# A recurrent attention and rational MLP kernel: first ScalarE activation made a reciprocal root, and a new order table

## The chip, the cores and the metric

The program runs on one core of one Trainium2 chip. The metric is device microseconds of one execution, the median of several. Every engine of the core (TensorE, VectorE, ScalarE, GpSimd, SyncE; in the rows PE, DVE, ACT, POOL, SP) works through its own list of instructions in order and waits on semaphores for the others.

## The reference

A gated linear recurrence over 768 steps for 4 batches of 8 heads of 48, and then an MLP with a rational function on its 3072 rows of 384:

```python
for t in range(S):
    state = alpha[:, :, t, :, None] * state + np.einsum('bhd,bhe->bhde', k[:, :, t], v[:, :, t])
    y[:, :, t] = np.einsum('bhd,bhde->bhe', q[:, :, t], state)
...
h = x @ w_in
h2 = h * h
h3 = h2 * h
P = a[0] + a[1] * h + a[2] * h2 + a[3] * h3
Q = 1.0 + np.abs(b[0]) * np.abs(h) + np.abs(b[1]) * h2
g = P / (Q + 1e-06)
return (g @ w_out).astype(np.float32)
```

The weights arrive as 64-bit floats and are turned into 32-bit ones on the chip.

## The kernel before

The 3072 tokens are cut into 24 blocks g of 128 for the recurrence and into 6 groups of 512 for the MLP, which does 96 jobs u: 10 small early ones on 256 tokens ("plain") and 86 wide ones, each of one slice of 128 of the 2048 hidden columns.

All work is split into 2672 steps. Each is recorded with an engine and with the steps that it must follow; the table ORDER then gives one sequence for all engines, and a bit in each entry moves a step to its other engine where it has one. No engine reorders its list, so a step that waits holds up all that stand behind it on that engine.

The steps that the prediction speaks of, by the names in the code:

- Loads on SP: `nat` (the first four blocks of alpha, k, q, 384 KB each for a pair of blocks), `w` (one of 16 tiles of weights, 768 KB), `ld` (from block 4 on: alpha, k or q of one block in four quarters, each two transfers of 48 KB into one buffer for alpha, `raw_a`, and one for k and q, `raw_qk`), `v`. The built program gives the transfers eight semaphores in turn, so a transfer is issued only when the one eight places ahead of it has landed. The notes of the change call this the ring.
- Weights: `low` and `join` on DVE, `abs` and `sign` on ACT (or POOL, DVE) turn a tile's 64-bit words into 32-bit floats.
- Recurrence of block g: `tn` (PE turns the loaded data) and `cp` (ACT copies it to SBUF) for the first four blocks; `ta` (alpha) and `tqk` (k and q), transposes on DVE, for the others; they free the one buffer for the next block's `ld`. Then `suf`, `inv`, `pre` (scans on DVE), `k` and `q` (products on POOL or DVE), `s` (scores, PE), `se` (ACT), `sm` (POOL), `kt` (PE), `ke` (ACT), `am` (PE), `kv` (DVE), `xh` and `xl`.
- MLP job u: `in` (PE, two halves 0 and 1), `ah`, `t1`, `q1` (ACT; `q1` also POOL), `qm` (POOL), `t2`, `t3` (DVE), `ars` (ACT, the reciprocal root, L755), `sq` (ACT), `p`, `t`, `g` (DVE, the last is L771), `gh` (ACT), `gl` (POOL or DVE), then `oh` and `ol` (PE). `in` of job u writes the PSUM bank that job u-3 used, so it must follow `g` of job u-3.
- `prime` (ACT) is an activation on one column whose result nobody uses. `one_eps`, its input, is a column that POOL sets at the start.

Of the kernel before, what the change touches and what calls it, by code (L numbers as in the profile page):

```python
# [24 lines left out]
class Plan:  # L25
# [52 lines left out]
    '^&j=3^D2}IP&mz_sW^#>tGnv8ilB*9LPgRvY^HLllIpUW96X<@si`!I+Nl}XM@^yOw15J1O-;v{IGU!>7+OSM)hw)`N~',
    'ytWA<f3=)I$AGH3QYvSbD4q(hQn|x7Ay<gr2EFG?QAY#k7`|(mOSa7U4bhLKUWQw2ao#OZ7^<SAA7;^<CXjv+09cP90P',
    '$wTEh{74%%Kr;WjLaRYT!n`sk0RiD*L+DlJVdo>T|(0trN-_%^%M<diKIuJZWEx<QwHT6?NRk+$p3$d&Er%uyi?4&-aG',  # L80
    'qi@b(SF)a{nZzBhz`;YI!sIOw;HC3&|kHa&Jx2%g>Zz<(NX%Pg4HehPwgTFw`qWi3g?55QBk@;$EmaG5{L#P)kPYp?$8',
    'R{O(#eI;E#Gqmq<fOhz{M=aCMI^Qy_4K3`BvG^os7%Ra%NY)K9exAJ8=lQm5!XC4g?~HC?BN^oV}Y4f61Ye$rza6nIO^',
    'k)WpvQK=wOg{mj?o*blsl~{~=sdsdf62VjYMTymKiUBd<8GWFSlo(>cCwfkCA&DwZ7LvecN(*sdl=?%x14$tTMBx{dG!',
    'T`)&?<}vUnwk*jHB^C`bMcCIxCLFF*rH@rPT<G92;Wt8q5aqA+;(DvAG~51mcXqycXkd0a%A|IXQf%^(dTzQ*sVY2Jv_',
    'Urs2#=b9}a3f^tAkPRj{673YKqRgw&+QMn)?=jL4OxD<O%&G|STXMn7b4)Q~3PRzL>J!jx;n1mB?+CU!8$YnVn<mZi8h',
    'BI*%m6tbRAxO$uRUIzJ1$YZ?#tK{pMysuunG14VF3;PsB9Bp7xDw}9S-B8rfy|JN3v*>IMTJ!nF3Jr!J6GYVkO@jtRo;',
    'PJxjr}Kv4LV-oQtT&oF2MyHEzQ7xExgH65NQJau3c9&A2=?=kDBs|KsXV0ZKv*E*fabCAk#z=E^EB4CmHRlY4S49?v5<',
    'z{Q~kjO1S2hg)$TsLdhVnuEA6PvAD(kK1xJs0jTznD^mC9>67_imC~dxEM_4fm{@(@J=iO?RX(i<tnfXL%Ab&=G{1r_h',
    '1;8hDE#=^Qb{Qox{03ci|aaHLxECa|AbnNS?`~cnOz<A-tG3^H9zkXbZD=>B!l<g_m<1IDm7w3=QL>yp>1u3T~{LKvUS',
    'pwP7bO<72pz>%kaq1#@{7kL7WEj92q^Zlc!k4z2|Aco)}&`Fw(#!2&+crPW$4OU>aVU+2?&hAYE5KE(}SH}ByMTt>BrI',  # L90
    '&cv8@_IhY`*<VY;D&IH_j5Za8>j`FxM|=Jp63JH18(t4zQ7l`KHTKHe4Fp^5q!l*@g85|gCk#aW4O<U_zgec+UhsI=ZA',
    'cl2f-u$!-w%LAK^OcI9}!t{FpoNKkfoo809ZVmv>w@@R5~}T;=ZYiJ$NZ1o_M{WGIxQFZ`8RM4oai=>^wVOK&hT5Uiw>',
# [1079 lines left out]
```

## Time and profile before

| | us |
|---|---|
| median of 3 runs | 535.96 |
| lowest and highest | 534.93 to 538.28 |
| the profiled execution, device time | 537.53 |
| its span, first to last instruction | 535.8 |

The rows further down come from the profiled execution, and their times count from the start of its span. Its device time is 1.7 us longer than its span, and 1.57 us over the median. TensorE's granted clock was 0.997 of full speed over the span.

### The profile page before, as it was taken

How to read it: one execution, taken by the hardware profiler on the slowest of the kernel's cores; microseconds unless marked ns; L12 is line 12 of the kernel's file. 1: busy time of each engine (PE TensorE's matmuls, PEld its weight loads, DVE VectorE, ACT ScalarE, POOL GpSimd, SP SyncE). 2: the span in 40 equal slices, each digit the busy share in tenths (PEclk: the TensorE clock that was granted, in tenths of full speed). 3: DMA queues.
4: the chain of work that ended last, by engine and by line, in shares of the span. 5: the costliest groups of instructions: out<-in, count | busy, mean ns of one | idle time of the engine just before them, and what ended most of it. 6: DMA issues, size and time to landing. Idle time of an engine off the chain costs nothing.

```text
span 535.8 us, 11861 instructions
## 1 busy us (share of the span) xinstructions
PE 517.1 (97%) x4342; PEld 428.1 (80%) x4342; DVE 480.7 (90%) x716; ACT 430.2 (80%) x730; POOL 392.4 (73%) x387
## 2 busy tenths in 40 slices
...
GB/s 246 260 249 219 214 229 116 116 140 113 128 140 117 92 127 71 104 96 109 92 68 87 112 73 94 97 87 59 128 95 55 88 83 18 1 40 1 59 1 62
DMA packets 146174, 57.46 MB, mean 107 GB/s; under 512 B 133056, under 2 KB 138688, under 8 KB 146112
## 3 DMA queue, kind: packets, MB, share of 16 engines
...
## 4 chain that ended last, share of the span: by engine, by line
PE 70%; SPq 7%; DMA 7%; DVE 6%; POOL 4%; ACT 3%; issue 2%; DVEq 0%; POOLq 0%; ACTq 0%
PE ps L670 29%; PE ps L689 23%; PE ps L683 6%; PE ps L547 5%; SPq L402 4%; PE ps L505 3%; DMA wo_words<-in_moe_w_out_dram 2%; DMA raw_a<-in_alpha_dram 2%; PE ps L656 1%; SPq L409 1%; DMA tv<-in_v_dram 1%; POOL gh_gl L778 1%; PE ps L523 1%; PE ps L566 1%; DVE t L748 1%
## 5 line engine op out<-in xcount | busy, mean ns | idle before, releaser
L670 PE MATMUL ps<-x,wi 128*128 128x512 f32 x774 | 209.1, 396 | 3.7 <-DVE t L771 3.7
L689 PE MATMUL ps<-gh_gl,wo 128*128 128x512 f32 x630 | 176.5, 400 | 0.1
L670 PEld LDWEIGHTS ps<-x,wi 128*128 128x128 f32 x774 | 143.8, 188 | 36.1 <-ACT ah L725 3.0
L737 POOL TENSOR_TENSOR qm<-qm,ah 128x512 f32<-128x512 f32 x96 | 124.2, 1295 | 24.7 <-ACT qm L734 14.7
L689 PEld LDWEIGHTS ps<-gh_gl,wo 128*128 128x128 f32 x630 | 115.5, 188 | 27.6 <-DVE parts L704 0.5
L778 POOL TENSOR_TENSOR gh_gl<-t,gh_gl 128x512 fp32r<-128x512 f32 x74 | 96.2, 1301 | 16.4 <-ACT gh_gl L774 6.3
L728 ACT ACTIVATE t<-ps,coef 128x512 f32<-128x512 f32 x96 | 74.5, 776 | 21.2 <-PE ps L670 12.8
L755 ACT ACTIVATE ps<-qm,one_eps 128x512 f32<-128x512 f32 x96 | 66.3, 691 | 20.5 <-POOL qm L737 11.9
L732 POOL TENSOR_SCALAR qm<-ah,bab 128x512 f32<-128x512 f32 x62 | 47.8, 771 | 47.4 <-ACT ah L725 22.5
L762 DVE SCALAR_TENSOR_TENSOR t<-t,coef,ps 128x512 f32<-128x512 f32 x96 | 71.0, 739 | 12.6 <-ACT ps L758 11.7
L748 DVE TENSOR_TENSOR t<-t,ps 128x512 f32<-128x512 f32 x96 | 65.1, 678 | 11.3 <-ACT t L728 5.6
L752 DVE SCALAR_TENSOR_TENSOR t<-t,coef,ps 128x512 f32<-128x512 f32 x96 | 71.3, 744 | 2.5 <-ACT ah L725 0.7
L725 ACT ACTIVATE ah<-ps 128x512 f32<-128x512 f32 x96 | 57.0, 593 | 17.7 <-PE ps L670 12.0
L771 DVE SCALAR_TENSOR_TENSOR t<-ps,t 128x512 f32<-128x512 f32 x96 | 66.1, 688 | 1.9
L765 DVE SCALAR_TENSOR_TENSOR ps<-qm,ps 128x512 f32<-128x512 f32 x96 | 66.0, 688 | 0.0
L774 ACT ACTIVATE gh_gl<-t 128x512 fp32r<-128x512 f32 x86 | 53.7, 628 | 9.2 <-DVE t L771 7.3
L758 ACT ACTIVATE ps<-ps 128x512 f32<-128x512 f32 x96 | 56.1, 585 | 2.0
L488 POOL TENSOR_TENSOR tqk<-tqk,tg 128x512 f32<-128x512 f32 x21 | 27.2, 1294 | 13.4 <-DVE tg L461 7.7
L491 POOL TENSOR_TENSOR tqk<-tqk,fp 128x512 f32<-128x512 f32 x21 | 27.2, 1295 | 12.6 <-DVE wo_words L274 5.0
L516 POOL TENSOR_SCALAR_AFFINE_SELECT sc<-sc 128x1024 f32<-128x1024 f32 x24 | 26.2, 1092 | 13.2 <-ACT sc L512 4.0
L461 DVE TENSOR_TENSOR_SCAN tg<-ta,ps 128x528 f32<-128x528 f32 x24 | 29.8, 1244 | 6.5 <-ACT ta L445 6.5
L683 PE MATMUL ps<-wo,gh_gl 128*128 128x384 f32 x180 | 35.5, 337 | 0.0
...
## 6 DMA issues: line engine op xcount, KB each, us to landing
...
wi_words<-in_moe_w_in_dram SPq DMA_DIRECT2D x8, 768.0 KB, 6.9
wo_words<-in_moe_w_out_dram SPq DMA_DIRECT2D x8, 768.0 KB, 7.0
...
```

Of the source, the lines that this page charges most:

```text
L670: nc.tensor.matmul(h_of(u), w(key)[:, kt * FU + f % FU, :], x[:, kt, xp, :], start=(n == 0), stop=(n == len(todo) - 1),)
L683: nc.tensor.matmul(bank(T_BANKS[tt], DM), g[:, tt * P : (tt + 1) * P], w(("o", f // FU))[:, f % FU, :], start=(f == 0 and first_w), stop=( ...
L689: nc.tensor.matmul(bank(O_BANKS[dt]), w(("o", f // FU))[:, f % FU, dt * P : (dt + 1) * P], g, start=(f == 0 and first_w), stop=(f == NF - ...
L728: nc.scalar.activation(buf(s, "t1", u), h_of(u), AF.Identity, bias=a2, scale=a3)
L737: nc.gpsimd.tensor_tensor(buf(s, "qm", u), buf(s, "qm", u), buf(s, "ah", u), op=ALU.mult)
L748: nc.vector.tensor_tensor(t, t, h_of(u), op=ALU.mult)
L752: nc.vector.scalar_tensor_tensor(t, t, a1, h_of(u), op0=ALU.add, op1=ALU.mult)
L755: nc.scalar.activation(h_of(u), buf(s, "qm", u), AF.Abs_reciprocal_sqrt, bias=one_eps)
L762: nc.vector.scalar_tensor_tensor(t, t, a0, h_of(u), op0=ALU.add, op1=ALU.mult)
L765: nc.vector.scalar_tensor_tensor(h_of(u), buf(s, "qm", u), 1.0 + 1e-6, h_of(u), op0=ALU.add, op1=ALU.mult)
L771: nc.vector.scalar_tensor_tensor(t, h_of(u), 2.0, t, op0=ALU.subtract, op1=ALU.mult, reverse0=True)
L778: eng.tensor_tensor(buf(s, "gl", u).rearrange("p a b -> p (a b)"), buf(s, "t1", u), gh, op=ALU.subtract)
```

## The change

`prime` becomes the function that `ars` uses, in place of a copy, and the four kinds of ACT steps that can come early (`bab`, `abs`, `sign` and `cp`) are now recorded as following it. The table is new: every engine's list is in another order, and 90 steps are on another engine than before.

```diff
 ORDER = [
-    'c-jTQ17ICU6ac_|TGh5~+qP}n_VqVuSlhO3+qP}n?aho+O2t*N)f6>RMOCPrnxI5QQC^K#anw{5T`f?H)k-y8O;eN9WH',
...
+    'c-jrs1Cu7a5<uZ}r#tCnZQHhO+qP|g`_9ac*0yciwr$%s?)?j=o~omiQ&AMFaVoBgtx!!-(bWWHlvh#Jc(p*qP!rWO6-UK',
...
-    add("bab", "ACT", 0.2, abs_coef, (), ["coef"])
+    add("bab", "ACT", 0.2, abs_coef, (), ["coef", "prime"])
...
-    add("prime", "ACT", 1.5, nc.scalar.activation, (first_act, one_eps, AF.Copy), ["one_eps"])
+    add("prime", "ACT", 1.5, nc.scalar.activation, (first_act, one_eps, AF.Abs_reciprocal_sqrt), ["one_eps"])
...
-        add(("abs", key), "ACT", 0.94, join_scale, (key, n), [("w", key)] + [("join" if kept(x) else "lo", x) for i, x in enumerate(keys[:n]) if wr_slot(i) == wr_slot(n)][-1:], alt=("POOL", 2.22, False))
+        add(("abs", key), "ACT", 0.94, join_scale, (key, n), [("w", key), "prime"] + [("join" if kept(x) else "lo", x) for i, x in enumerate(keys[:n]) if wr_slot(i) == wr_slot(n)][-1:], alt=("POOL", 2.22, False))
...
-        add(("sign", key), "ACT", 1.95, join_sign, (key,), [("low", key)], alt=("DVE", 1.04, True))
+        add(("sign", key), "ACT", 1.95, join_sign, (key,), [("low", key), "prime"], alt=("DVE", 1.04, True))
...
-                        [("tn", m, nm, x) for x in range(2) if par in (None, x)] + into[nm])
+                        [("tn", m, nm, x) for x in range(2) if par in (None, x)] + into[nm] + ["prime"])
```

The lines of the changed file are one lower than those of the file before (L770 there is L771 here).

**ScalarE at the start.** Before, the list begins with the load of a function table and the copies of what PE has turned. A second table load stands before the first `ars`.

```order
L445 ACT_TABLE_LOAD
L445 ACTIVATE ta0_82<-ps_69 128x4x128
L445 ACTIVATE ta1_83<-ps_69 128x4x128
L445 ACTIVATE tqk0_88<-ps_69 128x512 x2
L445 ACTIVATE tqk1_89<-ps_69 128x512
```

Now `prime` (L62) is first, and the list has this one table load and no other:

```order
L62 ACT_TABLE_LOAD
L62 ACTIVATE first_act_75<-one_eps_73 128x1
L444 ACTIVATE ta0_82<-ps_69 128x4x128
L444 ACTIVATE ta1_83<-ps_69 128x4x128
L444 ACTIVATE tqk0_88<-ps_69 128x512
L444 ACTIVATE tqk1_89<-ps_69 128x512
```

The table load stood behind a wait for PE's first turned data, and now stands ahead of all of it.

**VectorE around `ta` of block 7.** Before, from `pre` of block 6 on (`ta1` is the tile of block 7, `tqk0` that of block 6, `t11` and `t12` the working tiles of jobs 7 and 8; L453 is `ta`, L458 `tqk`, L771 `g`):

```order
L473 SCALAR_TENSOR_TENSOR fp0_84<-ta0_82,ps_69 128x528
L762 SCALAR_TENSOR_TENSOR t11_106<-t11_106,coef_71,ps_69 128x512
L748 TENSOR_TENSOR t12_107<-t12_107,ps_69 128x512
L765 SCALAR_TENSOR_TENSOR ps_69<-qm1_109,ps_69 128x512
L453 STREAM_TRANSPOSE ta1_83<-raw_a0_80 128x4x2x2x32
L771 SCALAR_TENSOR_TENSOR t11_106<-ps_69,t11_106 128x512
L752 SCALAR_TENSOR_TENSOR t12_107<-t12_107,coef_71,ps_69 128x512
L458 STREAM_TRANSPOSE tqk0_88<-raw_qk0_81 128x16x2x32
```

Now, from `g` of job 7 on (L770 is `g`, L457 `tqk`, L452 `ta`):

```order
L770 SCALAR_TENSOR_TENSOR t11_106<-ps_69,t11_106 128x512
L751 SCALAR_TENSOR_TENSOR t12_107<-t12_107,coef_71,ps_69 128x512
L457 STREAM_TRANSPOSE tqk0_88<-raw_qk0_81 128x16x2x32
L273 TENSOR_SCALAR wo7_words_983<-wo7_words_983 128x768
L293 SCALAR_TENSOR_TENSOR parts_76<-parts_76,wi7_words_828 128x768
L293 SCALAR_TENSOR_TENSOR parts_76<-parts_76,wo5_words_904 128x768
L761 SCALAR_TENSOR_TENSOR t12_107<-t12_107,coef_71,ps_69 128x512
L747 TENSOR_TENSOR t10_105<-t10_105,ps_69 128x512
L764 SCALAR_TENSOR_TENSOR ps_69<-qm0_108,ps_69 128x512
L751 SCALAR_TENSOR_TENSOR t10_105<-t10_105,coef_71,ps_69 128x512
L770 SCALAR_TENSOR_TENSOR t12_107<-ps_69,t12_107 128x512
L452 STREAM_TRANSPOSE ta1_83<-raw_a0_80 128x4x2x2x32
```

`ta` of block 7 stood ahead of `g` of job 7 and now follows `g` of job 8, eleven steps later.

**SyncE between two weight tiles.** Before, from `w` o1 to `w` o2:

```order
L257 DMA wo_words<-in_moe_w_out_dram 128x2x768
L402 DMA raw_qk_81<-in_k_dram 32x4x96 x2
L402 DMA raw_a_80<-in_alpha_dram 32x4x96 x6
L402 DMA raw_qk_81<-in_k_dram 32x4x96 x2
L257 DMA wo_words<-in_moe_w_out_dram 128x2x768
```

Now, from `w` o1 on:

```order
L256 DMA wo_words<-in_moe_w_out_dram 128x2x768
L448 DMA tv_93<-in_v_dram 128x8x48
L253 DMA wi_words<-in_moe_w_in_dram 128x3x512
L401 DMA raw_a_80<-in_alpha_dram 32x4x96 x2
L401 DMA raw_qk_81<-in_k_dram 32x4x96 x2
L401 DMA raw_qk_81<-in_q_dram 32x4x96 x2
L256 DMA wo_words<-in_moe_w_out_dram 128x2x768
```

Ten small transfers stood between these two weight tiles; now, from `w` o1 to `w` i7, no more than six stand between two. Further on, `w` o7 and o5 stood between the loads of block 5 and those of block 6's k and q; now o5 stands ahead of the first of block 6's k and q and o7 behind the first two quarters, and block 6's set is complete before any quarter but one of block 7's alpha. At the very start `w` i0 is the fourth transfer, ahead of `nat` of the second pair's alpha, where it was the fifth.

## Rows read from the trace of the kernel before

**Rows 1.** Page, busy time of each engine, its share and its instructions.

```profile
PE 517.1 (97%) x4342; PEld 428.1 (80%) x4342; DVE 480.7 (90%) x716; ACT 430.2 (80%) x730; POOL 392.4 (73%) x387
```

**Rows 2.** Busy time by stage; the first number after the stretch is its length.

```profile
9.10:43.00 33.90, 27.20 (x434) 25.21 (x432) 31.00 (x44) 27.66 (x44) 13.42 (x19) 0.95 0.94 255
43.00:107.00 64.00, 59.59 (x516) 49.19 (x517) 58.74 (x88) 57.61 (x78) 42.21 (x38) 1.00 0.67 177
107.00:164.00 57.00, 57.00 (x501) 46.11 (x501) 55.27 (x83) 53.34 (x89) 53.53 (x46) 1.00 0.52 126
164.00:245.00 81.00, 80.54 (x659) 64.56 (x658) 76.97 (x114) 66.31 (x118) 70.05 (x65) 1.00 0.44 103
245.00:529.00 284.00, 282.50 (x2167) 233.23 (x2166) 256.27 (x385) 222.38 (x401) 210.54 (x194) 1.00 0.31 67
```

**Rows 3.** PE, waits up to 107 us: total, times, longest.

```profile
PE ps L670 <- DVE t L771: 2.7, 1, 2.7
PE ps L547 <- ACT kt L526: 2.6, 1, 2.6
```

**Rows 4.** DVE, waits from 9.2 to 107 us.

```profile
DVE ta L453 <- DMA raw_a<-in_alpha_dram: 2.6, 1, 2.6
DVE tqk L458 <- DMA raw_a<-in_alpha_dram: 2.2, 1, 2.2
DVE st_s L576 <- PE ps L566: 1.4, 1, 1.4
DVE wi_words L294 <- ACT wr L266: 1.1, 1, 1.1
```

**Rows 5.** Timeline of ACT and DVE at the start: start, length.

```profile
7.14 1.28 ACT L445 ACT_TABLE_LOAD   x1 [7.14 <-PE ps L426]
8.43 1.09 ACT L445 ACTIVATE ta<-ps 128x512 f32<-128x512 f32 x2
9.12 2.40 DVE L461 TENSOR_TENSOR_SCAN tg<-ta,ps 128x528 f32<-128x528 f32 x2 [6.49 <-ACT ta L445]
```

**Rows 6.** Timeline of ACT at the first `ars`.

```profile
34.11 0.80 ACT L728 ACTIVATE t<-ps,coef 128x512 f32<-128x512 f32 x1
34.93 1.28 ACT L755 ACT_TABLE_LOAD   x1
36.22 0.69 ACT L755 ACTIVATE ps<-qm,one_eps 128x512 f32<-128x512 f32 x1
```

**Rows 7.** Timelines of DVE and PE around `ta` 7, `g` 7, `g` 9.

```profile
92.55 0.71 DVE L453 STREAM_TRANSPOSE ta<-raw_a 128x512 f32<-128x512 f32 x1 [2.62 <-DMA raw_a<-in_alpha_dram]
...
105.60 0.69 DVE L771 SCALAR_TENSOR_TENSOR t<-ps,t 128x512 f32<-128x512 f32 x1
...
93.99 1.41 PE L670 MATMUL ps<-x,wi 128*128 128x512 f32 x5 [2.65 <-DVE t L771]
...
106.49 0.73 PE L670 MATMUL ps<-x,wi 128*128 128x512 f32 x2
```

**Rows 8.** Groups by line: `gl`, `sign`, `q`, `k` on DVE, `q1` on ACT.

```profile
L734 ACT ACTIVATE qm<-ah,bab 128x512 f32<-128x512 f32 x34 | 27.6, 811 | 0.3
...
L778 DVE TENSOR_TENSOR gh_gl<-t,gh_gl 128x512 fp32r<-128x512 f32 x12 | 8.2, 684 | 1.0 <-issue 0.7 <-POOL sc L516 0.2
...
L280 DVE TENSOR_SCALAR wi_words<-wi_words 128x768 uint16<-128x768 uint16 x4 | 4.8, 1204 | 0.0
...
L491 DVE TENSOR_TENSOR tqk<-tqk,fp 128x512 f32<-128x512 f32 x3 | 3.2, 1053 | 0.0
...
L488 DVE TENSOR_TENSOR tqk<-tqk,tg 128x512 f32<-128x512 f32 x3 | 2.1, 690 | 0.1
```

**Rows 9.** The queue of SP: what its issues waited for, whole span.

```profile
SPq L402 <- DMA wo_words<-in_moe_w_out_dram: 8.9, 6, 3.5
```

**Rows 10.** Issues of 0 to 8 us: KB, us to landing.

```profile
wi_words<-in_moe_w_in_dram SPq DMA_DIRECT2D x1, 768.0 KB, 6.8
...
raw_second<-in_alpha_dram SPq DMA_DIRECT2D x1, 384.0 KB, 5.3
```

More of the change, by code (lines that the diff above doesn't have):

```diff
@@ L78 @@
[L78 to L92, printed above, removed]
@@ new lines @@
+    '6m$8q6X<oDn#c{1N1~Zt{SKjI;ZNUtEuj~e&DQ{jN$r%8mu3whN_1iq9b%MHC|7_o;shdp{}bdD!-nfd+E@SMk-7X)#ua=',
+    'Ra0eG!}LYfM-|YQRiyq;-&D8M2{lh2Q@PY6T|!O8`MQ}Jsf(-OdKOO9({KisQ~`Zojnbp_Oq{C6=*c0|ahkrSs;epbfhwh',
+    '@>vn2}?x$L)nR<a<6fzs1s#&_A9;?^t*Q$^nrx)ray05yeI;dBwy;`bg>vg)LTCC^bOI1sCQiIhp{Z_5l8$*`s@9Ld;q8_',
+    'U~dX6rv_v*WWJ8FdvQk(R9wNl?x&(vJKL4QzlvANo;SLv4Oo9e8dtD&k(U=hAh{nZw|PjA)p@Q3=UPU~&@K*$+AA4P?zR_',
+    'dVstoG~GdVpGhZ`2|EQEk_2^bXxs4N(j6upXv%>a!YQF)qO)dYArB-O@*Ou)3|!=_2}=J|A*H|4{%0$904nsG`7dby4ru-',
@@ new lines @@
+    'PA92LU&h}^a?zw?`Q>o6~iZWS>Fq}tBdO2DiFA$ALy6*iyEP>>YvJkfor;ldZq7c3)l5ObxOa{5A{;~p`$`HSca+9pulpx',
+    'p`$}$^;$pD8U)^kti(7lQiZC=+QB>BQ-!G~dX!3{-s@uer;ZOdbs~7GKj>#Vjfx8&^(P&L5<o8%0}?|#D6XSYOh^SuAZg&',
+    'U{-t9>EO@Sy!XN!Yrwy#awD3j$)~O*4M5E}m8dC&))ye3eP6#n57Oll~s3-$uR<Y@?{-(nNF)7>sV<4@;bda3lPzutN5s2',
+    'baDk=<2S>d}*2JvV;#;25Ir~vd1l+alqQl+8Pv;i$8pd65vGC@MhK{+WU<f5D)R8l90Qk01DLpmx=j&ebI%A!2whTK#T5>',
+    'pw<Lxo@?W`^{THIQ4Cr3|zQ^HN62N0}%I<)?C#l<H6c+J>2_AZ^CNsse4n>`;*kQF$r?Td@)qgUU2o)uqBzMCF0)SW0K1J',
@@ new lines @@
+    'gN%Sr&3TFib4@8t+P^9+JV`qA=RV2(3MI+H7WzysT_2p22>J?QhCS+jcAN28u*WfQ*|mv)u1>vrY2N^DnN1QPGbWVp(*Xd',
+    'o+C=qPHaX2>P20B4{A;|Mzo+H3Z|CSifYmbst&zrJoTXoREt7s7xtxoR25p&B-(>}u`Gm8P3TWyRGY$S01c$dstvWJynzU',
+    '+4O6KG45CPCN4v2ROr(Xhhz8R%T0&LSNZOCfX%tN!(UD54%`}Co1{PCiYERRt3e<wiFoO<Y89kG>&=6_>vuG$afvwb7jUG',
+    '`SX46tyMk{DL4Wp(ohUQRN-3%&0LzqirsV<D8qqLGb(JE@9j$w0HO~+^rl~LR1AP$7%w3F(=32GYHL2KzG?V?ser)V9mr?',
+    'P?5R0rnKeA-QW=nP$_8?=`W;aS>8=V$?Kp#9Va4r6=RNC&7f+@!W}i;mz+I!Nc~6?LK8)DG^_QM^E}skYigZ|EZ3qqig8(',
```

91 lines of the change are left out of this document (45 added, 46 removed).

## The prediction

> **What bounds the kernel now.** I read the page's busy times first [rows 1]: TensorE is busy for 97% of the span and VectorE for 90%. Over the whole run this looks like a kernel bound by matmuls, in which a new order can win nothing. So I cut the span by stage [rows 2]. From 107 to 529 us PE is busy for 57.00, 80.54 and 282.50 us of 57, 81 and 284, that is idle for 2.0 us in all. From 9.1 to 107 us it is idle for 6.70 + 4.41 = 11.1 us. Whatever an order can win lies ahead of 107 us, and what is won there stays won if PE is fed afterwards as it is now.
>
> Who holds PE up in that stage? VectorE: it is busy for 31.00 of 33.9 and 58.74 of 64 us [rows 2], its full 97.9 us but for 8.2. PE waited for `g` (DVE L771), 2.7 us in one piece [rows 3], and where no wait is shown it still follows `g`: `g` of job 9 starts at 105.60 and lasts 0.69, and `in` of job 12 starts at 106.49, 0.2 us after its end [rows 7]. Since PE rewrites the bank of job u-3 only after that job's `g`, the time of `g` 9 on DVE sets the time at which PE's closed stretch begins. So the sum is made on DVE's list up to `g` 9: when it starts, how much work stands in it, and how long it waits.
>
> The waits are four, 7.3 us together [rows 4]: `ta` of block 7 for its alpha (2.6), `tqk` of block 5 for its k and q (2.2), `kv` 2 for `am` 2 on PE (1.4), and a `join` for its `abs` on ACT (1.1).
>
> **The start.** DVE's first scan waits for ACT's first copy, and that copy for a table load of 1.28 us which begins only when PE's turned alpha is there [rows 5]. The load's instruction carries the wait of the copy behind it. With `prime` first, the load runs while the loads of alpha are under way, and the copy can start at 7.14 in place of 8.43: **1.3 us** earlier for DVE. The second table load (34.93, 1.28 us [rows 6]) goes too. ACT's list gains it, but DVE only as far as it waits for ACT, so it is counted with the waits. In the trace the load costs its 1.28 us and no more: the ACTIVATE ahead ends at 34.91, the one behind starts at 36.22 [rows 6]. The Trainium skill (ScalarE: Activation LUTs, What ACT_TABLE_LOAD costs) puts each switch at about 1.28 us of load and 1.38 of drain, 2.66 in all. By that the start would gain 2.7 us and the total of this forecast would be 529.6; the trace shows the load alone, so I give that 2 in 100, inside the better case below.
>
> **DVE's work ahead of `g` 9.** Counting both lists up to that step, five steps stood there and do not now: `sign` of i2, i4 and o3, `k` 2, `d` 2. Five stand there now and did not: `sign` of o0 and i3, `q` 1, and two totals. That is one `sign` less at 1.20, one product less at 0.69 against one more at 1.05 [rows 8], `d` less (as an elementwise product of three quarters of that width, some 0.5 by the 0.69) and two totals more, each between nothing and the 0.69 of a whole product; with 8 columns in place of 512 I take 0.2. 1.20 + 0.69 - 1.05 + 0.5 - 0.4 = **0.9 us** less.
>
> **The waits.** Each of the four has another step order in front of it now.
> - `ta` 7 stands eleven steps later, behind `g` 7 and `g` 8 and `tqk` 6 and two `join`. At 0.7 to 1.2 us each that is some 7 us or more, against a wait of 2.6. `g` 7 no longer stands behind it, so the 2.65 us of PE in front of `in` 10 [rows 7] has lost its cause.
> - `tqk` 5 has five more steps ahead of it (three `low` and two `join`; net of the 0.9 above some 2 us), and its loads are no longer stuck: SP waited six times, 8.9 us, for a w_out tile in order to issue a 48 KB quarter [rows 9], since a transfer goes out only when the one eight places ahead has landed. Ten small ones behind `w` o1 meet that wait; six do not.
> - `kv` 2 has `t2` 2, `g` 0 and `t3` 2 ahead of it now, 2 us against a wait of 1.4.
> - The `join` of i4 has its `abs` on POOL, and ACT is rid of the load of 1.28 just ahead.
>
> All four gone would be 7.3 us. What is late next is the reload of the one k and q buffer: block 7's and 8's eight quarters are issued only after `tqk` of the block before, and the new order brings `tqk` 7 nearer to `tqk` 6. And PE cannot follow without end: in 43 to 107 us it has only 4.4 us of idle time [rows 2], so with DVE 1.3 + 0.9 = 2.2 us ahead, `in` 12 can come 2.2 + 4.4 = 6.6 us earlier at most, plus what PE gains ahead of 43 us. The bounds are thus 2.2 us (all the waits come back under other names) and 6.6. I take **5.5**, nearer to the upper end, because the two load waits alone (4.8) each lose their cause outright, and after 107 us PE shows that it can run without a gap.
>
> **Behind 107 us.** The table moves work too: from POOL to DVE come, net, five `gl` (0.68) and three `q` (1.05), less one `k` (0.69) and one `lo` (taken as 1.0, between a product and a `sign`): 5 x 0.68 + 3 x 1.05 - 0.69 - 1.0 = 4.9 us, and to ACT twelve `q1` (0.81, 9.7 us) [rows 8]. ACT has 422 - 342.0 = 80 us of idle time after 107 us, and DVE 27.7 after 245 us [rows 2]: nothing there. From 107 to 245 us DVE has 1.7 + 4.0 us idle [rows 2], and the new list has some 3 us more up to `g` 24 (three `gl`, a `q` and an earlier `pre`, less one `gl` and one `lo`). Bounds: nothing, and 3 us. PE's list has its later `in` further back too, so I take **0.5 us** lost. At the end of the program the last twelve `oh` and `ol` follow the last `in`, where eleven did; a wait there would cost some tenths.
>
> **Sum.** 5.5 - 0.5 = 5.0 us. The profiled execution would go from a span of 535.8 to 530.8 and from 537.53 to 532.5 us. It was 1.57 us over the median of the runs, so I predict 535.96 - 5.0 = **531.0 us**.
>
> **Rivals.**
> - The waits come back: the reload of k and q, or `abs` and `sign` on ACT, which was busy 27.66 and 57.61 us of 33.9 and 64 [rows 2], take the place of the four. Then only 2.2 us are left, less 0.5: 534.3. For it: ACT is nearly full too. Against it: ACT loses two loads, 2.6 us.
> - The better case: nothing new waits, PE takes all that it can, and the late stage loses nothing: 6.6 and up to 2 us from ahead of 43 us, where PE was idle for 6.7 us and its granted clock was 0.95 [rows 2]. 535.96 - 8 = 528.
> - The start does not do what it says: `w` i0 now stands ahead of the second pair's alpha. Before, that alpha was issued at 3.2 and landed 5.3 later, at 8.5, and i0, issued at 4.55, 6.8 later, at 11.4 [rows 10]; i0 takes 2.9 us of the queue. PE turns that alpha ahead of `s` 0, so moved behind i0 it lands at about 11.4 and holds `s` 0 until it is turned. If it comes a microsecond or two later still, `am` 0 and behind it `kv` 0 hold DVE, and the 1.3 us are lost: 532.3.
> - Slower than before: DVE becomes the bound after 107 us. Its 5 us of added work find 1.7 us of idle time up to 164 and 4.0 up to 245; if they lengthen the run by 4 while the front gains only 2.2, the time is 535.96 + 1.8 = 537.8. It decides if PE loses over 3 us to waits between 107 and 245 us, where it now loses 0.5. Against it: DVE's idle time in [rows 2] takes it up.
>
> **How the numbers follow.** Forecast 0.52, waits back 0.17, better case 0.15, start undone 0.08, slower 0.08. A measurement of this kernel can tell about 1% (5.4 us) from no change, and the forecast lies just inside that line, at 530.6. Of the forecast's own range, 528.5 to 534, rather under half lies beyond the line; with the better case that makes faster 0.43. The slower case reaches +1% (541.3) only if the front gains nothing as well: slower 0.04. Within 1%: 0.53. The range from 526.8 to 536.0 takes in all but the slower case and the far ends of the others.
>
> **What would show it.** One table load in ACT's list, ended before 5 us, and the first copy at about 7.1; DVE's first scan at 7.8; no DVE wait for alpha at `ta` 7 and for k and q at `tqk` 5 over half a microsecond; `g` 9 at about 100 and `in` 12 at about 101; PE without a gap of over 1 us from there to the end. It is wrong if `in` 12 starts after 104, or if PE is idle for over 5 us after 107.

## The result: about 3 us slower, and the profile after

| | before | after |
|---|---|---|
| median of 8 runs, us | 536.24 | 539.86 |
| lowest and highest | 534.93 to 538.28 | 537.42 to 541.01 |
| the profiled execution, device time / span | 537.53 / 535.8 | 541.01 / 539.3 |
| granted clock in the profiled execution | 0.997 | 0.990 |

The ratio is 1.0055, with an interval of 1.003 to 1.008: by it 2.9 us slower (the medians lie 3.6 apart), where 5 us faster was forecast. That is within 1% of no change, but outside the range of 526.8 to 536.0. Each ratio further down is against runs of before from the same set. The profiled execution of after is its slowest of eight, and its TensorE ran at half clock for longer than before's. Over the timed runs the clocks are alike (a mean of 0.994 over after's eight runs, 0.993 to 0.994 over the four later sets of before's), so the clock is not what makes after slower.

The page's busy times, to be laid beside [rows 1]:

```profile
PE 522.3 (97%) x4342; PEld 431.7 (80%) x4342; DVE 489.4 (91%) x727; ACT 438.5 (81%) x738; POOL 388.5 (72%) x367
```

The stages of after, in the columns of [rows 2]:

```profile
9.10:43.00 33.90, 28.22 (x444) 25.92 (x442) 33.27 (x43) 25.96 (x42) 20.75 (x20) 0.97 0.95 266
43.00:107.00 64.00, 60.13 (x494) 50.32 (x495) 61.98 (x87) 57.66 (x77) 47.84 (x40) 0.94 0.68 172
107.00:164.00 57.00, 56.28 (x507) 44.81 (x507) 54.36 (x82) 49.17 (x81) 52.58 (x44) 1.00 0.52 120
164.00:245.00 81.00, 80.96 (x650) 65.28 (x649) 76.17 (x115) 67.72 (x120) 65.00 (x56) 1.00 0.45 100
245.00:529.00 284.00, 283.13 (x2176) 232.72 (x2175) 258.44 (x395) 233.06 (x414) 198.09 (x179) 1.00 0.33 69
```

DVE was idle for 8.16 us of the first two stages; now it is idle for 0.63 + 2.02 = 2.65. So 5.5 us of idle time are gone, and yet PE's closed stretch did not begin earlier in this run. The busy times of DVE and POOL tell where to look: DVE is busy for 5.5 us more with 130 instructions in place of 132, and POOL for 20.75 us in place of 13.42 and 47.84 in place of 42.21. DVE had less to do and took longer over it.

What DVE and PE waited for up to 107 us in after (total, times, longest), against [rows 3, 4]:

```profile
DVE t L761 <- ACT ps L757: 1.0, 2, 0.5
DVE tqk L457 <- DMA raw_a<-in_alpha_dram: 0.7, 1, 0.7
...
PE ps L546 <- ACT kt L525: 3.9, 1, 3.9
PE ps L669 <- DVE t L770: 1.9, 1, 1.9
```

The four waits of [rows 4] are gone; the longest left is 0.7. PE still waits for `g` (L770 now, 1.9 in place of 2.7), and for `ke` 3.9 in place of 2.6.

The same lines, `low`, `join` and `t2`, as groups of 9 to 107 us on DVE and `q1` on POOL; first before (L274, L294, L748, L732), then after (L273, L293, L747, L731):

```profile
L274 DVE TENSOR_SCALAR wi_words<-wi_words 128x768 uint32<-128x768 uint32 x8 | 4.7, 588 | 0.0
L294 DVE SCALAR_TENSOR_TENSOR wo_words<-wr,wo_words 128x768 uint32<-128x768 uint32 x3 | 2.9, 971 | 0.0
L294 DVE SCALAR_TENSOR_TENSOR parts<-parts,wi_words 128x768 uint32<-128x768 uint32 x2 | 1.9, 944 | 0.0
L748 DVE TENSOR_TENSOR t<-t,ps 128x512 f32<-128x512 f32 x11 | 7.5, 686 | 0.0
...
L732 POOL TENSOR_SCALAR qm<-ah,bab 128x512 f32<-128x512 f32 x6 | 4.6, 770 | 10.0 <-DVE wi_words L274 2.9 <-DVE wr L294 2.7 <-DVE wo_words L294 2.7
```

```profile
L273 DVE TENSOR_SCALAR wi_words<-wi_words 128x768 uint32<-128x768 uint32 x8 | 6.8, 853 | 0.3 <-DMA wi_words<-in_moe_w_in_dram 0.3
L293 DVE SCALAR_TENSOR_TENSOR wo_words<-wr,wo_words 128x768 uint32<-128x768 uint32 x3 | 3.9, 1306 | 0.0
L293 DVE SCALAR_TENSOR_TENSOR parts<-parts,wi_words 128x768 uint32<-128x768 uint32 x2 | 3.0, 1492 | 0.0
L747 DVE TENSOR_TENSOR t<-t,ps 128x512 f32<-128x512 f32 x10 | 6.7, 675 | 0.2 <-ACT t L727 0.2
...
L731 POOL TENSOR_SCALAR qm<-ah,bab 128x512 f32<-128x512 f32 x9 | 10.6, 1172 | 8.7 <-ACT ah L724 3.8 <-DVE parts L293 2.2 <-DVE wr L293 2.0
```

`low` lasts 853 ns in place of 588 and `join` 1306 and 1492 in place of 971 and 944, and POOL's `q1` 1172 in place of 770, while `t2`, one of whose operands lies in PSUM, lasts 675 in place of 686. Not every group is longer: `low` on `wo_words` lasts 650 in place of 561, and five small groups of `join` stay between 939 and 950. So it depends on where a step stands. In the timeline of after one such place is seen, DVE first, then POOL:

```profile
71.52 0.55 DVE L273 TENSOR_SCALAR wo_words<-wo_words 128x768 uint32<-128x768 uint32 x1
...
72.64 1.79 DVE L273 TENSOR_SCALAR wi_words<-wi_words 128x768 uint32<-128x768 uint32 x1
74.35 1.58 DVE L293 SCALAR_TENSOR_TENSOR wo_words<-wr,wo_words 128x768 uint32<-128x768 uint32 x1
```

```profile
72.19 1.82 POOL L313 TENSOR_TENSOR wi<-parts,wi 128x768 fp32r<-128x768 f32 x1 [1.67 <-ACT wi_words L277]
73.97 1.15 POOL L528 TENSOR_TENSOR st_d<-st_s,tot 128x384 f32<-128x384 f32 x1
75.10 2.26 POOL L731 TENSOR_SCALAR qm<-ah,bab 128x512 f32<-128x512 f32 x1
```

One `low` with POOL idle: 0.55. The next starts 0.45 after POOL's `lo` (L313) and ends 0.42 after it: 1.79. The `join` behind it ends 0.81 after POOL's `d` (L528).

To measure this over the whole stage I made a ledger of DVE's 128 steps from its first scan to `g` 9. "Work" gives each step a usual length of its kind, start to next start, low among those of both traces; "lengthening" is what it took beyond that; "waits" is idle time. What is called usual is a choice: with another one, work and lengthening shift against each other by about 1 us, alike in both kernels, and the difference in lengthening stays between 7.6 and 7.8. In us:

| kernel | first scan | `g` 9 | work | lengthening | waits |
|---|---|---|---|---|---|
| before | 9.12 | 105.60 | 86.99 | 1.59 | 7.90 |
| after | 8.87 | 106.45 | 85.81 | 9.41 | 2.36 |

Start 0.25 earlier, work 1.2 less, waits 5.5 less, lengthening 7.8 more: `g` 9 comes 0.85 later.

### The profile page after: what moved, and what is told of

Its sections match the earlier page's. It is cut to its first block, busy times and chain, and to the rows that moved or that the text cites. A ratio compares the mean times of both kernels' runs of the same rounds, so it can differ in the third digit from the quotient of the medians.

```text
span 539.3 us, 11866 instructions
## 1 busy us (share of the span) xinstructions
PE 522.3 (97%) x4342; PEld 431.7 (80%) x4342; DVE 489.4 (91%) x727; ACT 438.5 (81%) x738; POOL 388.5 (72%) x367
## 4 chain that ended last, share of the span: by engine, by line
PE 56%; DVE 11%; SPq 11%; DMA 6%; ACT 6%; POOL 5%; issue 4%; DVEq 0%; POOLq 0%; ACTq 0%
PE ps L669 22%; PE ps L688 16%; SPq L401 8%; PE ps L682 6%; PE ps L546 3%; PE ps L655 3%; PE ps L504 3%; POOL qm L736 2%; DMA tv<-in_v_dram 2%; PE ps L642 2%; DMA wi_words<-in_moe_w_in_dram 2%; SPq L408 2%; DMA raw_a<-in_alpha_dram 1%; DVE t L761 1%; DVE ps L764 1%
## 5 line engine op out<-in xcount | busy, mean ns | idle before, releaser
L669 PE MATMUL ps<-x,wi 128*128 128x512 f32 x774 | 201.8, 399 | 3.2 <-DVE t L770 3.2
L688 PE MATMUL ps<-gh_gl,wo 128*128 128x512 f32 x630 | 164.6, 398 | 0.0
L777 POOL TENSOR_TENSOR gh_gl<-t,gh_gl 128x512 fp32r<-128x512 f32 x69 | 89.9, 1305 | 29.7 <-ACT gh_gl L773 13.9
L747 DVE TENSOR_TENSOR t<-t,ps 128x512 f32<-128x512 f32 x96 | 64.9, 678 | 5.8 <-ACT t L727 4.5
L770 DVE SCALAR_TENSOR_TENSOR t<-ps,t 128x512 f32<-128x512 f32 x96 | 65.8, 686 | 1.5
L731 POOL TENSOR_SCALAR qm<-ah,bab 128x512 f32<-128x512 f32 x50 | 42.4, 848 | 32.5 <-ACT ah L724 17.7
L487 POOL TENSOR_TENSOR tqk<-tqk,tg 128x512 f32<-128x512 f32 x23 | 32.5, 1412 | 12.0 <-ACT tqk L444 6.8
L733 ACT ACTIVATE qm<-ah,bab 128x512 f32<-128x512 f32 x46 | 37.3, 813 | 2.7 <-DVE ta L469 1.3
L682 PE MATMUL ps<-wo,gh_gl 128*128 128x384 f32 x180 | 33.9, 338 | 0.0
L682 PEld LDWEIGHTS ps<-wo,gh_gl 128*128 128x128 f32 x180 | 31.8, 188 | 1.4 <-ACT gh_gl L773 0.2
```

What stands on the lines that cost most here:

```text
L669: nc.tensor.matmul(h_of(u), w(key)[:, kt * FU + f % FU, :], x[:, kt, xp, :], start=(n == 0), stop=(n == len(todo) - 1),)
L682: nc.tensor.matmul(bank(T_BANKS[tt], DM), g[:, tt * P : (tt + 1) * P], w(("o", f // FU))[:, f % FU, :], start=(f == 0 and first_w), stop=( ...
L688: nc.tensor.matmul(bank(O_BANKS[dt]), w(("o", f // FU))[:, f % FU, dt * P : (dt + 1) * P], g, start=(f == 0 and first_w), stop=(f == NF - ...
L747: nc.vector.tensor_tensor(t, t, h_of(u), op=ALU.mult)
L770: nc.vector.scalar_tensor_tensor(t, h_of(u), 2.0, t, op0=ALU.subtract, op1=ALU.mult, reverse0=True)
L777: eng.tensor_tensor(buf(s, "gl", u).rearrange("p a b -> p (a b)"), buf(s, "t1", u), gh, op=ALU.subtract)
```

## The experiments

Tables are rows of code that tell a reader nothing, so edits of the order are shown as the engine's list, or as which table gives which part. `in` 12 stands for the start of `in` of job 12, which is 106.49 in before and 109.10 in after.

**The start by itself.** Before's table, with the first activation changed and moved to the head.

```diff
-    add("prime", "ACT", 1.5, nc.scalar.activation, (first_act, one_eps, AF.Copy), ["one_eps"])
+    add("prime", "ACT", 1.5, nc.scalar.activation, (first_act, one_eps, AF.Abs_reciprocal_sqrt), ["one_eps"])
```

> The table of before, with one difference: the first activation of ScalarE is the reciprocal root and its entry (with that of its input) stands at the head of the table. Theory of the prediction: the first copy starts when the first turned alpha is there, 1.3 us earlier than with a table load in between, VectorE's first scan with it, and the time falls by about 1.3 us. Rival: TensorE's clock at the start differs from run to run by up to 1.1 us of work (4.40 us for the rise before, 6.74 after) and VectorE's later waits take back the rest: the time falls by 0 to 0.7 us.

Measured 1.0009 (0.9992 to 1.0025): no change. The first copy starts at 7.49 and the first scan at 8.17, 0.95 earlier, and the first `ars` at 33.83 in place of 36.22. `in` of job 3 is 3.6 us ahead, `in` of job 6 0.95, and `in` 12 is not ahead (106.62). DVE ran up to the loads and waited there:

```profile
DVE tqk L458 <- DMA raw_qk<-in_q_dram: 2.6, 1, 2.6
DVE ta L453 <- DMA raw_a<-in_alpha_dram: 2.1, 1, 2.1
DVE tqk L458 <- DMA raw_qk<-in_k_dram: 2.1, 1, 2.1
```

**Three moves.** After's table with the `join` of o0 seven steps later, the `low` of o6 seven earlier and POOL's `lo` of i5 three later. POOL's list:

```diff
-L313 TENSOR_TENSOR wi<-parts,wi 128x6x128
 L528 TENSOR_TENSOR st_d<-st_s,tot 128x384
 L731 TENSOR_SCALAR qm<-ah,bab 128x512
 L515 AFFINE_SELECT sc<-sc 128x1024
+L313 TENSOR_TENSOR wi<-parts,wi 128x6x128
```

> The changed kernel with three entries of its table moved: the join of o0 seven steps later and the low of o6 seven steps earlier on VectorE, the lo of i5 three steps later on GpSimd; nothing goes to another engine and TensorE, ScalarE and SyncE keep their lists. Port theory (VectorE's steps on weights and GpSimd's elementwise steps take turns; in the front of the changed kernel that lengthens VectorE's steps by some 9 us where it was 1.6 before): the lengthening up to g of job 9 falls by 2 to 4 us, in of job 12 starts 2 to 4 us earlier and the time is 2 to 4 us under the changed kernel's. Rival (TensorE at half clock after its own gaps, or the later stage, sets the time): within 0.7 us of the changed kernel.

Measured 1.0011 (0.999 to 1.0033), 0.0044 or 2.4 us under after's 1.0055, as expected of less lengthening. Lengthening 7.40 for 9.41, `in` 12 at 103.96. Those 5 us are one run against one run and cannot be put down to the moves: the clock was not low there in this run, and the kernel with the second table load (below), which has no moves, comes at 104.06 in such a run. And the lead did not reach the end. Behind 107 us DVE waits for block 8's k and q, and PE for `g`:

```profile
122.96 1.25 DVE L457 STREAM_TRANSPOSE tqk<-raw_qk 128x1024 f32<-128x1024 f32 x1 [2.64 <-DMA raw_qk<-in_k_dram]
...
128.37 1.55 PE L669 MATMUL ps<-x,wi 128*128 128x512 f32 x5 [1.79 <-DVE t L770]
```

**The lists of DVE and POOL ordered anew**, so that fewer of the lengthened steps stand beside POOL's (20 steps of DVE's list and 5 of POOL's stand elsewhere). The head of DVE's list:

```diff
-L469 RECIPROCAL ta<-tg 128x4
 L279 TENSOR_SCALAR wi_words<-wi_words 128x768
+L469 RECIPROCAL ta<-tg 128x4
 L472 SCALAR_TENSOR_TENSOR fp<-ta,ps 128x528
-L460 SCALAR_TENSOR_TENSOR tg<-ta,ps 128x528
 L293 SCALAR_TENSOR_TENSOR wi_words<-wr,wi_words 128x6x128
+L460 SCALAR_TENSOR_TENSOR tg<-ta,ps 128x528
```

> The changed kernel with VectorE's and GpSimd's lists up to about job 12 put in another order, so that fewer of VectorE's weight steps stand beside a GpSimd step; every step stays on its engine, and TensorE, ScalarE and SyncE keep their lists. Port theory: lengthening up to g of job 9 down from 9.4 to about 4 us, in of job 12 some 5 us earlier, at 104, the time about 535 beside 540 for the changed kernel. Rival (clock of TensorE or the later stage): in of job 12 may come earlier but the time stays within 1 us of the changed kernel's.

Measured 1.0025 (1.0004 to 1.0045), 537.82, some 1.6 us under after where 5 were expected: missed. Lengthening fell to 4.56, but 1.5 us of it came back as waits (3.87; the longest 2.1 for block 5's k and q), and `in` 12 at 103.80 is no earlier than with three moves. So lengthening is not a sum that can be taken off; part of it stood where DVE would have waited.

**Without the guard.** `Plan.run` lets a POOL step wait for the last of DVE's steps marked `lock` that stands ahead of it in the table, not the other way round. This kernel is after without that.

```diff
-                held = new[-1]
+                held = None
```

> The changed kernel with the same table, but the waits that make a GpSimd step follow the VectorE weight step ahead of it in the table are not made. Port theory: these waits are what kept such steps apart; without them VectorE's lengthening up to g of job 9 grows beyond 9.4 us and the time rises by 2 to 8 us. Rival (the waits only make GpSimd late and cost time themselves): faster than the changed kernel by 1 to 3 us.

Measured 1.0116 (1.0075 to 1.0157), 542.89, over four runs. Lengthening 12.27. So the guard is worth some 3 us (1.0116 against 1.0055, intervals that just touch), and the lengthening grows when POOL is held apart from DVE less.

**Three more moves**, on top of the three: `tqk` 8 behind `g` 13, the `join` of o7 ahead of `p` 13, `gl` 14 behind `g` 15. DVE's list:

```diff
-L457 STREAM_TRANSPOSE tqk<-raw_qk 128x16x2x32
 L751 SCALAR_TENSOR_TENSOR t<-t,coef,ps 128x512
-L761 SCALAR_TENSOR_TENSOR t<-t,coef,ps 128x512
 L293 SCALAR_TENSOR_TENSOR parts<-parts,wo_words 128x768
+L761 SCALAR_TENSOR_TENSOR t<-t,coef,ps 128x512
 L764 SCALAR_TENSOR_TENSOR ps<-qm,ps 128x512
 L761 SCALAR_TENSOR_TENSOR t<-t,coef,ps 128x512
 L770 SCALAR_TENSOR_TENSOR t<-ps,t 128x512
+L457 STREAM_TRANSPOSE tqk<-raw_qk 128x16x2x32
```

> The kernel with three moves, and three more on VectorE alone: tqk of block 8 behind g of job 13 instead of ahead of t3 of job 14, the join of o7 ahead of p of job 13, gl of job 14 behind g of job 15. In the run with three moves tqk of block 8 waited 2.6 us for its k and q and TensorE then 1.8 and 0.7 us for g of jobs 13 and 15. Theory (the lead won in front is given back to that load): both waits of TensorE go, about 2.5 us, and the time is near 534. Rival (VectorE is full there, the waits only change their names): within 0.7 us of the run with three moves, 536.4.

Measured 1.0023 (1.0008 to 1.0038): no better than three. `in` 12 is 1.7 us ahead of the kernel with three moves (102.23), `in` of job 18 0.67 (137.77). The wait for `g` 13 is gone and others stand in its place, for `xh` 7 and `xl` 7 ahead of `in` 16 and for `gl` 12 on POOL; the matmuls behind them ran at half clock (granted 0.72 from 128 to 134):

```profile
125.45 0.49 PE L669 MATMUL ps<-x,wi 128*128 128x512 f32 x1 [0.55 <-ACT x L592]
126.16 1.20 PE L669 MATMUL ps<-x,wi 128*128 128x512 f32 x4 [0.21 <-DVE x L607]
128.31 1.59 PE L688 MATMUL ps<-gh_gl,wo 128*128 128x512 f32 x3 [0.95 <-POOL gh_gl L777]
129.69 4.14 PE L669 MATMUL ps<-x,wi 128*128 128x512 f32 x13
```

**`w` i0 behind the second pair's alpha**, as the rival on the start wants it, else after. SP's list:

```diff
-L253 DMA wi_words<-in_moe_w_in_dram 128x3x512
 L408 DMA raw_second<-in_alpha_dram 128x8x96
+L253 DMA wi_words<-in_moe_w_in_dram 128x3x512
```

> The changed kernel with w of i0 back behind the alpha of the second pair on SyncE, nothing else. If the early weight tile is what ate the gain of the start, s of block 0 starts some 1.0 us earlier after the first scan (4.7 us as with the table of before, where the changed kernel took 5.4 to 5.8) and the time falls by up to 1 us. Port theory: VectorE's lengthening, not the start, sets the time of in of job 12; the time stays within 0.7 us of the changed kernel.

Measured 1.0043 (1.0025 to 1.0061), not told apart from after's 1.0055. `s` 0 comes 4.71 us after the first scan, in after 5.42.

**The second table load back**, else after:

```diff
-    add("prime", "ACT", 1.5, nc.scalar.activation, (first_act, one_eps, AF.Abs_reciprocal_sqrt), ["one_eps"])
+    add("prime", "ACT", 1.5, nc.scalar.activation, (first_act, one_eps, AF.Copy), ["one_eps"])
```

> The changed kernel with prime as a copy again, still first: one table load at the start, and the second one, 1.28 us, back ahead of the first ars. Port theory: in the changed kernel ScalarE stands idle for 2.6 us ahead of that ars (it waits for qm of job 0 on GpSimd), so the load is covered and the time stays within 0.5 us. Rival (the load delays all that follows): 1.3 us slower.

Measured 1.0053 (1.003 to 1.0076), not told apart from after's. The load ran from 34.20 to 35.48 and `qm` 0, which that `ars` waits for as well, ended at 34.61, so 0.4 of the 1.28 us is covered there, and the rest does not show in the time. In this profile the clock was full from 100 to 110 us and `in` 12 came at 104.06 with 8.37 of lengthening. So 5 us of after's 109.10 belong to its one run: 1.6 are PE at half clock behind `g` 9 (`in` 12 follows it by 2.0 there and by 0.4 here), 1.15 the later first scan (8.87 against 7.72 here), and the rest more lengthening and more waits on DVE.

**The lengthening by itself.** A kernel of 148 us that computes nothing of the reference (it writes zeros), profiled once, runs three DVE instructions of a kind alone, beside three products, three `q1`, three masks or three memsets of POOL.

```diff
+        nc.vector.tensor_scalar(pair[:, :, 0], pair[:, :, 0], 29, None, op0=ALU.logical_shift_right)
+        nc.gpsimd.tensor_tensor(ta[:, 0:512], ta[:, 0:512], tb[:, 0:512], op=ALU.mult)
```

> Another program, which computes none of the outputs and writes zeros: three instructions of one form on VectorE, alone and at the same time as three on GpSimd, for the forms join, low, sign, gl (operands in SBUF only), t2, g, xl (one operand in PSUM), beside a product like k, a q1, a mask like sm and a memset on GpSimd. Port theory (forms with all operands in SBUF take turns with GpSimd's): three join beside three products take about the sum, 3 x 0.87 + 3 x 1.28 = 6.5 us, and so low, sign and gl; t2, g and xl beside them take the longer of the two, 3.8 us. Rival (both only share bandwidth): all forms are stretched by a like share, those with PSUM too, and none reaches the sum.

Its timeline; L61 is `join`, L63 `low`, L67 `gl`, L69 `t2`; 5 to 17 us alone, 26 to 48 beside products, from 120 beside memsets:

```profile
5.37 2.88 DVE L61 SCALAR_TENSOR_TENSOR words<-wr,words 128x768 uint32<-128x768 uint32 x3
8.59 1.75 DVE L63 TENSOR_SCALAR words<-words 128x768 uint32<-128x768 uint32 x3 [0.33 <-ACT words L89]
...
26.14 5.90 DVE L61 SCALAR_TENSOR_TENSOR words<-wr,words 128x768 uint32<-128x768 uint32 x3 [2.78 <-ACT words L89]
32.36 4.28 DVE L63 TENSOR_SCALAR words<-words 128x768 uint32<-128x768 uint32 x3 [0.33 <-ACT words L89]
...
42.79 4.43 DVE L67 TENSOR_TENSOR t<-t,x 128x512 f32<-128x512 f32 x3 [0.42 <-ACT t L89]
47.55 2.13 DVE L69 TENSOR_TENSOR t<-t,ps 128x512 f32<-128x512 f32 x3 [0.33 <-ACT t L89]
...
120.42 2.95 DVE L61 SCALAR_TENSOR_TENSOR words<-wr,words 128x768 uint32<-128x768 uint32 x3 [5.14 <-ACT words L89]
123.69 3.89 DVE L63 TENSOR_SCALAR words<-words 128x768 uint32<-128x768 uint32 x3 [0.33 <-ACT words L89]
```

| three of | alone | beside products | `q1` | masks | memsets |
|---|---|---|---|---|---|
| `join` | 2.88 | 5.90 | 3.94 | 5.36 | 2.95 |
| `low` | 1.75 | 4.28 | 2.33 | 3.76 | 3.89 |
| `sign` | 3.12 | 5.40 | 3.74 | 5.16 | 4.95 |
| `gl` | 2.14 | 4.43 | 2.72 | 4.05 | 2.14 |
| `t2`, `g` | 2.13, 2.14 | the same | the same | the same | the same |

Steps with a PSUM operand are not touched; those with all in SBUF take up to 2.4 times as long. Three products alone last 3.94, and beside them three `join` take 5.90: short of the 6.82 of one behind the other, and far over the 3.94 of the longer of the two, so they mostly take turns, as expected. A like share for all, the rival, would have touched `t2` and `g`. The Trainium skill (SBUF — State Buffer, Who interferes with whom) says that a DVE instruction with two SBUF inputs contends with a GpSimd instruction that reads SBUF and not with one that only writes it, that one in a two-port mode contends with GpSimd too, and that the loser waits for the whole instruction. The table agrees for `join` and `gl`, with two SBUF inputs, which are not lengthened beside memsets (2.95, 2.14). `low` and `sign`, with one, are (3.89, 4.95), as in a two-port mode; in which mode they run no run here shows. The prediction did not weigh this rule.

**Front and rest apart.** Two kernels in which one table gives the steps up to the first half of `in` of job 14 and the other the rest.

```diff
 front_alone
-all from after's table
+up to `in` 14 from after's, the rest from before's
 late_alone
-all from after's table
+up to `in` 14 from before's with the start changed, the rest from after's
```

> The changed kernel's table up to the first half of in of job 14, and behind it the steps that are left in the order and on the engines of before. Port theory with a late loss (the new front gains only some 2 us because VectorE and GpSimd take turns, and the new rest then loses them and more): in of job 12 at about 104, the time 0 to 2 us under before. Rival (the new front itself is what is slower, the rest costs nothing): in of job 12 later than 106.5 and the time 2 to 4 us over before.

> The table of before with the reciprocal root first, up to the first half of in of job 14, and behind it the steps that are left in the order and on the engines of the changed kernel. Late-loss theory (seven steps and 4.3 us more of VectorE between g of jobs 9 and 24 than before, lengthening included): TensorE waits for g or xl between 107 and 170 us, 1.5 to 3.5 us, and the time is that much over before. Rival (the rest is as good as before's, only the front is slower): within 0.7 us of before.

The front: 0.9981 (0.9964 to 0.9998), 1.0 us faster; `in` 12 at 104.53, lengthening 8.88, waits 0.47. The rest: 1.0081 (1.0054 to 1.0109), more than expected; less the 0.0009 of the changed start that is 0.0072, 3.9 us slower. In its profiled run the loads at the start landed up to 1.1 us later than with the start alone, and DVE waited 1.4 for block 0, so the front of its trace is not used. -1.0 + 3.9 = 2.9, the whole of what was measured; that it comes out to the tenth is luck, since the intervals are 0.9 and 1.5 us to either side.

The clock has a part in the front. Its runs have a mean granted clock of 0.997, those of before in the same set 0.993; and the 19 runs of before, over all sets, that had 0.997 took a mean of 534.8, which is what the new front takes (534.85). Whether the order gives the clock or the clock the microsecond is open. The rest's 3.9 is not the clock (0.995).

**The best of both.** The front of the kernel with three moves, with `w` i0 behind the second pair's alpha, and before's order from `in` 14, or from `in` 9.

```diff
 joined_best
-up to `in` 14 from after's table, the rest from before's
+up to `in` 14 from three_moves' with alpha ahead of `w` i0, the rest from before's
 joined_best9
+the same, but up to `in` 9
```

> As the run of the new front alone, but its front has the three moves and w of i0 behind the alpha of the second pair. Both theories of the cause put together (less lengthening in front, none of the late loss): in of job 12 at 102 to 103.5, and the time 1.5 to 4 us under before, 532 to 534.5. Rival (VectorE and GpSimd are full after 107 us in before's order too and take any lead back): within 0.7 us of before.

> The same, with the change from the new order to that of before already at the first half of in of job 9. If before's order between jobs 9 and 14 is the better one (its VectorE weight steps stand mostly apart from GpSimd's), it is 0 to 2 us faster than the join at job 14; if its loads (the wait of ta of block 7, 2.6 us) take the lead back, it is 1 to 2 us slower than that and in of job 12 starts at 105 or later.

**0.9951** (0.9933 to 0.9969), 533.27: 2.6 us faster than before. `in` 12 at 103.08, lengthening 5.68, waits 2.10, and PE has no gap from 107 to 164. Its mean clock is 0.998, and its mean time of 533.35 is still 1.5 us under before's runs at 0.997. With the joint at `in` 9: 0.9976 (0.9954 to 0.9999); lengthening only 3.50, but waits are back (4.71, the longest 2.0 for block 7's alpha), with `in` 12 at 103.69.

**Where the rest loses.** The joined kernel with after's order in one part: from `in` 14 to `in` 18, from `in` 18, from `in` 24.

```diff
 new_14_18
+`in` 14 to `in` 18 from after's table, else joined_best
 new_from_18, new_from_24
+from `in` 18 (`in` 24) on from after's table, else joined_best
```

> The joined kernel (ratio to before 0.9951), with the steps from the first half of in of job 14 to that of in of job 18 in the changed kernel's order and on its engines; before's order only from there. If the late loss lies in that stretch (tqk of block 8 placed where it waits for its k and q, in of job 16 with too little work of TensorE between am of block 7 and itself, gl of job 14 on VectorE), the time is 1.5 to 3 us over the joined kernel, ratio 0.998 to 1.001, and TensorE shows waits of some 2.5 us ahead of in of jobs 16 and 18. Rival (the loss lies behind job 18): ratio within 0.001 of 0.9951.

> The joined kernel up to the first half of in of job 18, and from there the steps that are left in the changed kernel's order and on its engines. If the loss lies between jobs 14 and 18, the ratio stays within 0.001 of 0.9951. If it lies behind (VectorE's seven more steps up to g of job 24, and what follows), it is 0.998 or more.

> The same with the change of order at the first half of in of job 24. If nothing is lost behind job 24, the ratio stays within 0.001 of 0.9951; each 0.001 over that is 0.5 us lost there.

Jobs 14 to 18: 1.0019 (1.0 to 1.0039), 0.0068 or 3.6 us over the joined kernel. In the window from 107 to 164 the columns are those of [rows 2]; the joined kernel first, then this one, with its PE timeline at `in` 16 and PE's waits for `g`:

```profile
107.00:164.00 57.00, 57.00 (x501) 46.07 (x500) 54.40 (x84) 52.44 (x88) 53.17 (x45) 1.00 0.55 129
```

```profile
107.00:164.00 57.00, 54.37 (x483) 42.69 (x482) 52.70 (x80) 47.98 (x81) 51.03 (x44) 1.00 0.50 117
```

```profile
126.34 1.57 PE L669 MATMUL ps<-x,wi 128*128 128x512 f32 x5 [1.30 <-DVE t L770]
```

```profile
PE ps L669 <- DVE t L770: 2.0, 2, 1.3
```

PE loses 2.6 us there, 2.0 of it waiting for `g`, as it did with three moves. From `in` 24: 1.0026 (1.0012 to 1.004), 0.0075 or 4.0 us over the joined kernel, but PE's last instruction ends 0.69 us earlier than there; 3.0 of the loss lie behind it, where 7.1 us pass in place of 4.1 (at the end). In after's own run 4.3 pass there, so this loss is not after's. From `in` 18: 1.0155 (1.0127 to 1.0183), with PE waiting 5.1 us for `g` right at the joint, which neither whole table has; so it says nothing on jobs 18 to 24, and they stay open.

## Why the prediction was wrong

**Start, 1.3 us.** The mechanism was right: one table load, ended at 2.17, and the first copy then waits for PE alone. Alone it gave 0.95; in after's profiled run 0.25, for a reason on PE. ACT, DVE and PE of after at the start:

```profile
0.89 1.28 ACT L62 ACT_TABLE_LOAD   x1 [0.89 <-PEq L1155]
...
8.24 1.09 ACT L444 ACTIVATE ta<-ps 128x512 f32<-128x512 f32 x2 [5.85 <-PE ps L425]
...
8.87 1.25 DVE L460 TENSOR_TENSOR_SCAN tg<-ta,ps 128x528 f32<-128x528 f32 x1 [5.86 <-ACT ta L444]
...
1.51 4.53 PE L418 MATMUL ps<-ident 128*128 128x128 f32 x20 [1.51 <-POOL ident masks.py:199]
5.83 2.37 PE L425 MATMUL ps<-ident,raw_a 128*128 128x128 f32 x16
```

and PE of before:

```profile
1.51 3.80 PE L419 MATMUL ps<-ident 128*128 128x128 f32 x20 [1.51 <-POOL ident masks.py:199]
5.14 1.91 PE L426 MATMUL ps<-ident,raw_a 128*128 128x128 f32 x16
```

The same twenty matmuls began at 1.51, and the trace's record of the granted clock has the rise to full (2.4 GHz) at 4.41 in before and at 6.76 here. In the kernel with the second table load it rose at 4.42, as in before, and the first scan began at 7.72, 1.40 earlier: the size was right too, at a like clock; no run gained the 2.7 us that was given 2 in 100. Either way the gain went into the waits for loads: 1.0009 for the whole run.

**Work, 0.9 us less.** Measured 1.2 less. **Waits, all four gone.** Right: the four names are gone, and idle time is 5.5 us less. Neither was sized badly.

**The step that failed: "the sum is made on DVE's list up to `g` 9: when it starts, how much work stands in it, and how long it waits."** It takes a step to last as long in the new order as in the old. The new order puts the weights' steps on DVE beside POOL's `k`, `q`, `d`, `q1` and `lo`, and they take turns: 7.8 us more over the 128 steps. POOL's busy time in the first two stages, 13.0 us more for 3 instructions more, shows it from the other side: by the usual lengths some 4 of these are other work (three `q1`, a `k` and an `abs` more), and some 9 are steps that last longer. The probe shows which kinds and beside what, the kernel without the guard that more of it costs more, and the kernels with three moves, the new lists and the joint that less of it can be had. What the runs do not show is a sum: of the 4.9 us of lengthening that the new lists took off, 1.5 came back as waits.

**`in` 12 follows `g` 9 by 0.2 us.** Not in after's run: `g` 9 ended at 107.1 and `in` 12 began at 109.10. (In four runs of nearly the same order, named below, it follows by 0.4.)

```profile
101.54 3.58 PE L669 MATMUL ps<-x,wi 128*128 128x512 f32 x9 [1.91 <-DVE t L770]
104.91 3.17 PE L655 MATMUL ps<-t,wo_words 128*128 128x256 f32 x12
...
109.10 1.44 PE L669 MATMUL ps<-x,wi 128*128 128x512 f32 x5
```

After its waits PE was at half clock (granted 0.73 from 100 to 105), nine matmuls took 3.58 us, and PE was what was late. In the runs of nearly the same order whose clock was full there (three moves, `w` i0 moved, the second load, the front alone) `in` 12 came at 103.8 to 104.5, some 2 to 2.7 ahead of before's profiled run, which was itself 1.3 over its median. By the ratio the front is worth 1.0 us, not the 5.5 taken, and less than the lower bound of 2.2: the case that work grows by taking turns was in no bound.

**Behind 107 us, 0.5 us lost in bounds of nothing and 3.** By the ratio 3.9 (2.4 to 5.4). The spans say it as well: from `in` 12 to the end the five kernels with before's rest took 428.7 to 429.5 us, and six with after's rest 430.2 (after's own run, whose `in` 12 was late) to 432.7; the rest by itself took 431.7, and the kernel without the guard 434.1. The work that comes earlier was counted rightly, "some 3 us more up to `g` 24": 73.15 for 70.18, 2.97. What failed is the reason for taking the lower end, that DVE's idle time takes it up. It did not, because the idle time stands where DVE waits for something, with three moves 2.6 us for block 8's k and q, in after's run 1.0 for that load and 1.2 for ACT (2.97 us of waits became 2.53, beside 1.8 us more of lengthening). The loss that the runs place lies in jobs 14 to 18: `g` 13 and `g` 15 are not ready when PE's list comes to `in` 16 and 18. Three moves there changed the name of the wait, to `xh` 7, `xl` 7 and `gl` 12, and not the time.

**The rivals.** "Slower" came, by half its mechanism: the late stage costs 3.9 us, about the 4 that it gave, but its front of 2.2 was taken as safe, and it is 1.0. Its sign, over 3 us of waits on PE between 107 and 245 us, is met only without the guard: PE's idle time there is 0.8 us in after's run, 2.5 and 2.7 with three moves and with the second load, and 3.2 without the guard. "The waits come back" did not happen in after. "Start undone" was right that `s` 0 is held by 0.7 us and wrong that it counts: moving `w` i0 gave 1.0043 for 1.0055, within both intervals.

**Sum.** Front -1.0, rest +3.9: +2.9 us against -5.0. Of the 7.9 us between them 4.5 lie in the front (5.5 taken) and 3.4 behind it (0.5 taken).
